# An attention and MLP kernel on one core: later hardware transposes, five output buffers, batch 2 turned by TensorE, window blocks at stride 57, and one Gelu over two tiles

## The chip, the cores and the metric

The kernel runs on one core of one Trainium2 chip. The metric is the device time of one execution in microseconds (us). Each variant was executed several times, the changed ones in the same session on the same chip as the kernel before, and only runs in the normal fast state are compared. The granted clock is the share of TensorE's full clock that the profile shows as granted. Two runs were slow and are left out: one of the kernel before (425.46 us, mean granted clock 0.749) and one of a variant (334.4 us, where its other five lie between 327.21 and 330.06).

## The reference, cut to what matters

```python
# q, k, v: 8 batches x 8 heads x 576 positions x 64, fp32
q_d, k_d, v_d = means of four neighbours of q, k, v          # 144 positions
out_up    = repeat(softmax(q_d @ k_d.T / 8) @ v_d, 4)        # coarse attention, each row four times
out_local = softmax over |i-j| < 4 only (q @ k.T / 8) @ v    # a band of 7
x = (out_up + out_local) as [8*576, 512]                     # 4608 tokens
y = gelu(x @ w_in[512, 2048]) @ w_out[2048, 512]
```

## The kernel before

The 4608 tokens are worked in nine blocks `c` of 512. `m1(c)` is x @ w_in with the Gelu (64 matmuls of 512 columns), `m2(c)` is g @ w_out (another 64), and between the matmuls of `m2(c)` the attention of batch `c+1` is woven in, so that TensorE has work while the softmax of a head pair runs on ScalarE and VectorE. I call the work from the first matmul of `m1(c)` to the first of `m1(c+1)` the stage of block c. The "opening" is everything before block 1's stage: batch 0's attention, all of block 0, and batch 1's attention within it.

```python
def m1(c):
    t = ppool.tile([128, 1024], F32, tag="nm", name="m_first")   # first two tiles: one PSUM tile
    half = [t[:, 0:512], t[:, 512:1024]]                         # (block 0 takes two separate banks)
    for fcs in ((0, 1, 2), (3,)):
        for j in range(2):
            for fc in fcs:
                nc.tensor.matmul(out=half[j], ..., start=(fc == 0), stop=(fc == 3))
                if fc == 3:
                    nc.scalar.activation(out=g[:, j, :], in_=half[j], func=ACTF.Gelu)
    for j in range(2, NJ): ...      # fourteen more tiles, in two alternating banks

def m2(c):
    for t in range(4): ...          # 16 matmuls each, then:
        osb = wpool.tile([128, 512], F32, tag="osb", bufs=2, name="out_sb")
        (VectorE or ScalarE copy)(out=osb, in_=ps)
        nc.sync.dma_start(out=out[r0:r0 + 128, :], in_=osb)

def qk_cast(b): ...   # q, k of batch b to fp16 in DRAM (two GpSimd DMAs)
def qk_turn(b): ...   # two hardware transposes ("crossbar" below) DRAM -> SBUF, on SyncE's queue; for batches >= 2
def t_in_g(b, p, which): ...   # the same by TensorE for batch 1: 6 transposes and 6 sums of four
def prep(b): ...      # VectorE: key blocks kb, sums of four kdt, kdz and qd, then v_down(b)
def v_down(b): ...    # VectorE: v summed over four neighbours (two tensor_reduce), v_lm

for c in range(NCH):
    b = c + 1
    ...               # b == 1: t_in_g between the matmuls of m1; else prep(b)
    attn(b, f2)       # f2 issues m2(c)'s matmuls in between
    qk_turn(b + 2); v_load(b + 2); qk_cast(b + 3)
    f2()              # the rest of m2(c)
# [cut: masks, the opening's plan, scores, av, norm_out]
```

In the attention of a head pair, `scores` fills a PSUM tile, ScalarE takes exp, `mask` on VectorE multiplies by the band, and only then can `av` (whose first matmul is the `sc<-e,ON` of the profile) run.

The softmax here doesn't subtract the row's maximum and nothing guards it: scores larger than these inputs give would overflow.

Of the kernel before, what the change touches and what calls it, by code (L numbers as in the profile page):

```python
# [16 lines left out]
def kernel(  # L17
# [9 lines left out]
    nc = tc.nc  # L27
# [18 lines left out]
    WN = [58 * i for i in range(5)] + [280 + 58 * i for i in range(5)]  # L46
    QN = [0, 61, 119, 177, 235, 288, 341, 399, 457, 515]
    QL = [61, 58, 58, 58, 53, 53, 58, 58, 58, 61]
# [78 lines left out]
    def vw_load(b, src, ps=None):  # L127
        for p in ps or range(NP):
            for hh in range(2):
                for g in range(2):  # L130
                    x = src[2 * p + hh, 280 * g:280 * g + 64, :]
                    nc.gpsimd.dma_start(out=ld[b % 2]["vw"][64 * hh:64 * hh + 64, 5 * g:5 * g + 5, p, 64 * hh:64 * hh + 64],  # L132
                                  in_=bass.AP(x.tensor, x.offset, [[D, 64], [58 * D, 5], [1, D]]))
# [88 lines left out]
    def m1(c):  # L222
        g = wpool.tile([128, NJ, 512], F16, tag="gT", bufs=2, name="gT")
        gT[c] = g
        x0 = 512 * c % XR
        if c:
            t = ppool.tile([128, 1024], F32, tag="nm", name="m_first")
            half = [t[:, 0:512], t[:, 512:1024]]
        else:
            half = [mm(), mm()]  # L230
        for fcs in ((0, 1, 2), (3,)):
            for j in range(2):
                for fc in fcs:
                    nc.tensor.matmul(out=half[j], lhsT=w_in_sb[:, fc, 128 * j:128 * j + 128],  # L234
                                     rhs=xT[:, fc, x0:x0 + 512], start=(fc == 0), stop=(fc == 3))
                    if fc == 3:
                        nc.scalar.activation(out=g[:, j, :], in_=half[j], func=ACTF.Gelu)  # L237
                    yield
        for j in range(2, NJ):
            ps = mm()  # L240
            for fc in range(4):
                nc.tensor.matmul(out=ps, lhsT=w_in_sb[:, fc, 128 * j:128 * j + 128],  # L242
                                 rhs=xT[:, fc, x0:x0 + 512], start=(fc == 0), stop=(fc == 3))
                if fc == 3:
                    nc.scalar.activation(out=g[:, j, :], in_=ps, func=ACTF.Gelu)  # L245
                yield

    def m2(c):
        g = gT[c]
        for t in range(4):  # L250
            r0 = 512 * c + 128 * t
            if c == NCH - 1 and t == 3:
                for half in range(2):
                    cs = slice(256 * half, 256 * half + 256)
                    ps = mm()
                    for j in range(NJ):
                        nc.tensor.matmul(out=ps[:, 0:256], lhsT=g[:, j, 128 * t:128 * t + 128],  # L257
                                         rhs=w_out_sb[:, j, cs], start=(j == 0), stop=(j == NJ - 1))
                        yield
                    osb = wpool.tile([128, 256], F32, tag="osa", bufs=2, name="out_sa")  # L260
                    nc.vector.tensor_copy(out=osb, in_=ps[:, 0:256])  # L261
                    nc.sync.dma_start(out=out[r0:r0 + 128, cs], in_=osb)
                continue
            ps = mm()
            for j in range(NJ):
                nc.tensor.matmul(out=ps, lhsT=g[:, j, 128 * t:128 * t + 128],  # L266
                                 rhs=w_out_sb[:, j, :], start=(j == 0), stop=(j == NJ - 1))
                if j == NJ - 1:
                    osb = wpool.tile([128, 512], F32, tag="osb", bufs=2, name="out_sb")
# [5 lines left out]
    def k_blocks(p, tr):  # L275
        for hh in range(2):
            r = slice(64 * hh, 64 * hh + 64)
            x = tr[r]
            nc.vector.tensor_copy(  # L279
                out=kb[r, p, :, 64 * hh:64 * hh + 64].rearrange("q (g i) c -> q g i c", g=2),  # L280
                in_=bass.AP(x.tensor, x.offset, [x.ap[0], [280, 2], [58, 5], [1, 64]]))

    def prep(b):
        kt, qt = xT_of(b, "kn"), xT_of(b, "qn")
        with nc.allow_low_precision(reason="sums of four, kept in fp16 as before"):
            for p in range(NP):
                k_blocks(p, kt[:, p, :])
# [8 lines left out]
    def t_in_g(b, p, which):  # L296
        nat = nat6(ld[b]["qn" if which == "q" else "kn"])
# [11 lines left out]
        else:  # L309
            k_blocks(p, tr)  # L310
# [26 lines left out]
    def v_down(b):  # L337
        L = ld[b % 2]
        with nc.allow_low_precision(reason="sums of four, kept in fp16 as before"):
            nc.vector.tensor_reduce(out=L["vd"][:, :, 0:64], in_=L["vt"].rearrange("p h r d -> p h d r"),  # L340
                                    axis=AX.X, op=ALU.add)
            nc.vector.tensor_reduce(out=L["vls"], in_=L["vl"].rearrange("p r d -> p d r"), axis=AX.X, op=ALU.add)
# [21 lines left out]
    def scores(b, p):  # L364
# [4 lines left out]
        for j in range(NW):  # L369
            c = 512 * (j // 5) + QN[j] - SH * (j // 5)  # L370
            nc.tensor.matmul(out=sc[:, c:c + QL[j]], lhsT=kb[:, p, j, :], rhs=(qT0 if b == 1 else xT_of(b, "qn"))[:, p, QN[j]:QN[j] + QL[j]],  # L371
                             start=True, stop=True)
# [165 lines left out]
    def v_load(b):  # L538
        vg_load(b, v[b])
        vw_load(b, v[b])  # L540
# [118 lines left out]
    vg_load(1, v[1])  # L659
    for f in range(4):  # L660
# [3 lines left out]
    qk_cast(2)  # L664
    qk_turn(2)
# [15 lines left out]
    for c in range(NCH):  # L681
        b = c + 1
        f1 = filler(m1(c)) if c else f1_0
        if b == 1:
            f1(10)
            for p in range(NP):
                t_in_g(1, p, "k")
                f1(7)
                t_in_g(1, p, "q")
                f1(4)  # L690
            k_lo()
            v_down(1)
# [3 lines left out]
        elif b < B:  # L696
# [3 lines left out]
        if b < B:  # L700
            to_exp()
            attn(b, f2)
            if b + 2 < B:
                qk_turn(b + 2)
# [3 lines left out]
        f2()  # L708

# [29 lines left out]
```

## Time and profile before

| what | value |
|---|---|
| time, median of 3 runs | 349.85 us (349.38 to 349.9) |
| profiled span, mean granted clock | 349.3 us, 0.976 |
| opening (start to block 1's first matmul) | 85.38 us |
| stage of block 1; of a later block | 35.42 us; 33.54 us |
| from block 1's first matmul to the end | 263.9 us |

The last three rows are read from the start of the first `m_first` matmul of each block in TensorE's timeline; the same rows are given for every kernel below. (The chain of waits dates the same start up to 0.2 us later, since it counts from the end of the matmul before.) The prediction shows the hole before block 1 and the stages. What it only mentions is how block 0's attention starts. These are two pieces of the chain of waits (start, length, what):

```profile
50.83 3.69 DVE v_d L340
...
56.23 2.19 DVE v_win L693
58.43 0.32 DVE e L383
```

and TensorE's own timeline at the same place, where the bracket is the idle time before the group and what ended it:

```profile
57.62 1.01 PE L266 MATMUL m_ps<-w_out_sb,gT 128*128 128x512 f16 x2 [2.38 <-DMA w_out_sb<-in_moe_w_out_dram]
58.79 0.64 PE L389 MATMUL sc<-e,ON 128*128 128x288 f16 x2 [0.16 <-DVE e L383]
```

Two things must both be there before TensorE can go on: the last piece of w_out (57.62) and the first mask (58.75). I call them the two gates. They arrive within 1.2 us of each other.

### The profile page before, as it was taken

Reading aid. Unit: us, or ns where it says so; the run is one execution under the profiler, and the core shown is the slowest. Engines: PE = TensorE matmul, PEld = TensorE weight load, DVE = VectorE, ACT = ScalarE, POOL = GpSimd, SP = SyncE. Lnnn points to the kernel's source line nnn. Section 1 sums busy time; section 2 is a strip of 40 time slices with the busy share of each in tenths; the row PEclk is TensorE's granted clock in tenths of the full one; section 3 lists DMA queues with packets and bytes.
Section 4 is the critical chain, followed back from the end, with each engine's and each line's share of the span. In section 5 each row is a group of like instructions: output and inputs, shape, how many; then the busy total and the mean of one; then the engine's idle time right before and its main releaser. Section 6 shows DMA issues by size and latency. Waiting matters only on the chain.

```text
span 349.3 us, 6169 instructions
## 1 busy us (share of the span) xinstructions
PE 321.3 (92%) x2430; PEld 170.8 (49%) x2430; DVE 211.3 (60%) x378; ACT 224.6 (64%) x403; POOL 140.4 (40%) x184
## 2 busy tenths in 40 slices
PE   8998996952999999999999999999999999999995
PEld 4873453520356445644554456446544654444444
DVE  7797477713966695779878978893798470000000
ACT  7764354705678767876887687768877886514620
POOL 8957677568468348666278037300000000000000
PEclk9999898995999999999999999999999999999999
DMA  6999999999999999999999979900200020011012
GB/s 83 162 205 137 153 152 119 169 179 165 171 157 122 210 165 132 167 200 197 111 133 169 197 74 122 212 17 0 92 30 0 2 93 30 2 60 61 0 44 78
DMA packets 156157, 39.93 MB, mean 114 GB/s; under 512 B 138080, under 2 KB 151648, under 8 KB 156128
## 3 DMA queue, kind: packets, MB, share of 16 engines
q0 software_dynamic: 122768, 23.02, 82.4%
q1 hardware_dynamic: 33360, 16.52, 21.4%
q8 instruction: 19, 0.31, 0.4%
q14 instruction: 10, 0.08, 0.1%
HBM read 46.01 MB, written 16.52 MB: 179 GB/s over the span
## 4 chain that ended last, share of the span: by engine, by line
PE 75%; DMA 10%; DVE 5%; ACT 4%; POOL 2%; SPq 2%; issue 1%; ACTq 0%; POOLq 0%
PE m_ps L242 31%; PE m_ps L266 29%; PE m_first L234 5%; DMA w_in_sb<-in_moe_w_in_dram 3%; DMA out_dram<-out_sb 3%; DMA q_nat<-in_q_dram 2%; PE sc L371 2%; PE nm L399 2%; PE sc L389 2%; SPq L155 2%; ACT gT L237 1%; DVE v_d L340 1%; DMA k_nat<-in_k_dram 1%; PE m_ps L257 1%; POOL k_nat L122 1%
## 5 line engine op out<-in xcount | busy, mean ns | idle before, releaser
L266 PE MATMUL m_ps<-w_out_sb,gT 128*128 128x512 f16 x560 | 132.3, 380 | 2.9 <-DMA w_out_sb<-in_moe_w_out_dram 2.9
L242 PE MATMUL m_ps<-xT,w_in_sb 128*128 128x512 f16 x504 | 112.9, 382 | 0.5 <-ACT gT L237 0.5
L245 ACT ACTIVATE gT<-m_ps 128x512 f16<-128x512 f32 x126 | 75.3, 597 | 41.2 <-PE m_ps L242 41.2
L132 POOL DMA_DIRECT2D v_win<-in_v_dram x112 | 78.4, 819 | 51.6 <-DMA v_grp<-in_v_dram 14.9
L242 PEld LDWEIGHTS <-w_in_sb 128*128 128x128 f16 x504 | 48.9, 98 | 65.7 <-issue 9.7
L266 PEld LDWEIGHTS <-gT 128*128 128x128 f16 x560 | 51.2, 98 | 56.3 <-issue 3.7
L414 DVE TENSOR_TENSOR xl<-nm,lr 128x576 f16<-128x576 f32 x28 | 21.2, 758 | 39.6 <-ACT lr L410 39.6
L270 ACT COPY out_sb<-m_ps 128x512 f32<-128x512 f32 x21 | 12.3, 585 | 38.0 <-PE m_ps L266 23.2
L261 DVE COPY out_sa<-m_ps 128x256 f32<-128x256 f32 x2 | 0.8, 425 | 56.3 <-PE m_ps L257 56.3
L234 PE MATMUL m_first<-xT,w_in_sb 128*128 128x512 f16 x64 | 17.8, 405 | 16.5 <-DVE up L416 11.0
L340 DVE TENSOR_REDUCE v_d<-v_grp 128x512 f16<-128x2048 f16 x7 | 25.9, 3705 | 0.2
L383 DVE TENSOR_TENSOR e<-e,band 128x576 f16<-128x576 f16 x28 | 12.6, 451 | 21.6 <-ACT e L378 21.5
L426 DVE TENSOR_TENSOR xT<-xl,up 128x576 f16<-128x576 f16 (+8 forms) x41 | 22.1, 566 | 1.0
L279 DVE COPY kb<-k_nat 64x640 f16<-64x640 f16 x48 | 20.6, 430 | 0.6
L408 ACT ACTIVATE lr<-sc 128x576 f32<-128x576 f32 x28 | 18.4, 657 | 3.2 <-PE sc L389 3.2
L409 ACT ACTIVATE lr<-lr 128x576 f32<-128x576 f32 x28 | 19.1, 682 | 0.9
L377 ACT ACTIVATE ed<-sc 128x288 f16<-128x288 f32 x28 | 11.4, 406 | 11.9 <-PE sc L371 11.9
L137 POOL DMA_DIRECT2D v_grp<-in_v_dram x7 | 10.5, 1500 | 20.0 <-DVE v_d L340 20.0
L378 ACT ACTIVATE e<-sc 128x576 f16<-128x576 f32 x28 | 18.0, 644 | 0.0
L234 PEld LDWEIGHTS <-w_in_sb 128*128 128x128 f16 x72 | 7.1, 103 | 20.9 <-DVE up L416 12.4
L416 DVE TENSOR_TENSOR up<-nm,lr 64x144 f16<-64x144 f32 x56 | 16.5, 295 | 0.4
L150 POOL DMA_DIRECT2D q<-in_q_dram x6 | 16.6, 2771 | 0.0
(181 smaller groups left out, 434.2 us busy)
## 6 DMA issues: line engine op xcount, KB each, us to landing
out_dram<-out_sb SPq DMA_DIRECT2D x35, 256.0 KB, 2.7
v_win<-in_v_dram POOLq DMA_DIRECT2D x112, 40.0 KB, 5.8
v_grp<-in_v_dram POOLq DMA_DIRECT2D x7, 512.0 KB, 12.5
k<-in_k_dram POOLq DMA_DIRECT2D x6, 576.0 KB, 8.7
q<-in_q_dram POOLq DMA_DIRECT2D x6, 576.0 KB, 11.1
w_in_sb<-in_moe_w_in_dram POOLq DMA_DIRECT2D x4, 512.0 KB, 8.7
w_out_sb<-in_moe_w_out_dram POOLq DMA_DIRECT2D x4, 512.0 KB, 8.7
old<-in_v_dram POOLq DMA_DIRECT2D x5, 128.0 KB, 6.8
```

The lines of the kernel that those rows point to most:

```text
L132: nc.gpsimd.dma_start(out=ld[b % 2]["vw"][64 * hh:64 * hh + 64, 5 * g:5 * g + 5, p, 64 * hh:64 * hh + 64], in_=bass.AP(x.tensor, x.offset, ...
L234: nc.tensor.matmul(out=half[j], lhsT=w_in_sb[:, fc, 128 * j:128 * j + 128], rhs=xT[:, fc, x0:x0 + 512], start=(fc == 0), stop=(fc == 3))
L242: nc.tensor.matmul(out=ps, lhsT=w_in_sb[:, fc, 128 * j:128 * j + 128], rhs=xT[:, fc, x0:x0 + 512], start=(fc == 0), stop=(fc == 3))
L245: nc.scalar.activation(out=g[:, j, :], in_=ps, func=ACTF.Gelu)
L266: nc.tensor.matmul(out=ps, lhsT=g[:, j, 128 * t:128 * t + 128], rhs=w_out_sb[:, j, :], start=(j == 0), stop=(j == NJ - 1))
L279: nc.vector.tensor_copy(out=kb[r, p, :, 64 * hh:64 * hh + 64].rearrange("q (g i) c -> q g i c", g=2), in_=bass.AP(x.tensor, x.offset, [x.a ...
L340: nc.vector.tensor_reduce(out=L["vd"][:, :, 0:64], in_=L["vt"].rearrange("p h r d -> p h d r"), axis=AX.X, op=ALU.add)
L378: nc.scalar.activation(out=e.rearrange("p (g c) -> p g c", g=2), in_=sc2[:, :, 0:SH], func=ACTF.Exp, scale=0.125)
L408: nc.scalar.activation(out=lr2, in_=sc2[:, :, 0:SH], func=ACTF.Ln)
L409: nc.scalar.activation(out=lr2, in_=lr2, func=ACTF.Exp, scale=-1.0)
L414: nc.vector.tensor_tensor(out=xl.rearrange("p (g c) -> p g c", g=2), in0=nm2[:, :, 0:SH], in1=lr2, op=ALU.mult)
L426: nc.vector.tensor_tensor(out=xT[:, p, y:y + z - a].rearrange("p (g r) -> p g r", r=4), in0=xl[:, a:z].rearrange("p (g r) -> p g r", r=4), ...
```

## The change

Five edits, meant to take away the hole before block 1 and small waits elsewhere: five output buffers instead of two, and the two transposes issued after a stage's four outputs; batch 2 loaded and turned by TensorE like batch 1, so that no transpose is needed that early; ten windows at stride 57 (one load for nine, one for the tenth) instead of two runs of five at stride 58; `v_down` as pairwise adds instead of reduces, key blocks copied for all head pairs at once; and one Gelu over the first two tiles of each block after the first.

```diff
-    WN = [58 * i for i in range(5)] + [280 + 58 * i for i in range(5)]
+    WN = [57 * i for i in range(9)] + [512]
     ...
-                    if fc == 3:
+                    if fc == 3 and c == 0:
                         nc.scalar.activation(out=g[:, j, :], in_=half[j], func=ACTF.Gelu)
+                    elif fc == 3 and j == 1:
+                        nc.scalar.activation(out=g[:, 0:2, :], in_=t.rearrange("p (j c) -> p j c", j=2), func=ACTF.Gelu)
     ...
-                    osb = wpool.tile([128, 512], F32, tag="osb", bufs=2, name="out_sb")
+                    osb = wpool.tile([128, 512], F32, tag="osb", bufs=5, name="out_sb")
     ...            # the last two half outputs share this tag now
     def v_down(b):
-            nc.vector.tensor_reduce(out=L["vd"][:, :, 0:64], in_=L["vt"].rearrange("p h r d -> p h d r"), ...)
-            nc.vector.tensor_reduce(out=L["vls"], in_=L["vl"].rearrange("p r d -> p d r"), ...)
+        for x, o in (heads 0-3, heads 4-7, v_lo):        # [shortened]
+            nc.vector.tensor_tensor(out=t, in0=x[:, :, 0:2, :], in1=x[:, :, 2:4, :], op=ALU.add)
+            nc.vector.tensor_tensor(out=o, in0=t[:, :, 0, :], in1=t[:, :, 1, :], op=ALU.add)
     ...
-    qk_cast(2)
-    qk_turn(2)
+    run(load_qk(2))
     ...
-        if b == 1:
+        if b <= 2:
             ...      # t_in_g between the matmuls of m1, k_lo, v_down
-                qk_turn(b + 2)
                 v_load(b + 2)
             ...
         f2()
+        if b + 2 < B:
+            qk_turn(b + 2)
```

More of the change, by code (lines that the diff above doesn't have):

```diff
@@ L45 @@
     NW = 10
-    WN = [58 * i for i in range(5)] + [280 + 58 * i for i in range(5)]
-    QN = [0, 61, 119, 177, 235, 288, 341, 399, 457, 515]
-    QL = [61, 58, 58, 58, 53, 53, 58, 58, 58, 61]
+    WN = [57 * i for i in range(9)] + [512]
+    QN = [0] + [57 * i + 3 for i in range(1, 10)]
+    QL = [60] + [57] * 8 + [60]
     SH = S // 2
@@ L127, in vw_load, with vw_last @@
     def vw_load(b, src, ps=None):
+        vw = ld[b % 2]["vw"]
         for p in ps or range(NP):
             for hh in range(2):
-                for g in range(2):
-                    x = src[2 * p + hh, 280 * g:280 * g + 64, :]
-                    nc.gpsimd.dma_start(out=ld[b % 2]["vw"][64 * hh:64 * hh + 64, 5 * g:5 * g + 5, p, 64 * hh:64 * hh + 64],
-                                  in_=bass.AP(x.tensor, x.offset, [[D, 64], [58 * D, 5], [1, D]]))
+                x = src[2 * p + hh, 0:64, :]
+                nc.gpsimd.dma_start(out=vw[64 * hh:64 * hh + 64, 0:9, p, 64 * hh:64 * hh + 64],
+                                    in_=bass.AP(x.tensor, x.offset, [[D, 64], [57 * D, 9], [1, D]]))
+    def vw_last(b, src):
+        for hh in range(2):
+            nc.gpsimd.dma_start(out=ld[b % 2]["vw"][64 * hh:64 * hh + 64, 9, :, 64 * hh:64 * hh + 64],
+                                in_=src[hh:H:2, 512:576, :].rearrange("h s d -> s h d"))
     def vg_load(b, src):
@@ L259, in m2 @@
                         yield
-                    osb = wpool.tile([128, 256], F32, tag="osa", bufs=2, name="out_sa")
+                    osb = wpool.tile([128, 512], F32, tag="osb", bufs=5, name="out_sb")[:, 0:256]
                     nc.vector.tensor_copy(out=osb, in_=ps[:, 0:256])
@@ L272, in m2, with k_blocks @@
                 yield
-    def k_blocks(p, tr):
+    def k_blocks(ps, tr):
         for hh in range(2):
             r = slice(64 * hh, 64 * hh + 64)
+            o = kb[r, ps, :, 64 * hh:64 * hh + 64]
             x = tr[r]
-            nc.vector.tensor_copy(
-                out=kb[r, p, :, 64 * hh:64 * hh + 64].rearrange("q (g i) c -> q g i c", g=2),
-                in_=bass.AP(x.tensor, x.offset, [x.ap[0], [280, 2], [58, 5], [1, 64]]))
+            nc.vector.tensor_copy(out=o[:, :, 0:9, :], in_=bass.AP(x.tensor, x.offset, [x.ap[0], x.ap[1], [57, 9], [1, 64]]))
+            nc.vector.tensor_copy(out=o[:, :, 9, :], in_=x[:, :, 512:576])
     def prep(b):
@@ L285, in prep @@
         with nc.allow_low_precision(reason="sums of four, kept in fp16 as before"):
-            for p in range(NP):
-                k_blocks(p, kt[:, p, :])
+            k_blocks(slice(0, NP), kt)
             nc.vector.tensor_reduce(out=kdt, in_=kt.rearrange("p a (g r) -> p a g r", r=4), axis=AX.X, op=ALU.add)
@@ L296, in t_in_g @@
     def t_in_g(b, p, which):
-        nat = nat6(ld[b]["qn" if which == "q" else "kn"])
+        nat = nat6(ld[b % 2]["qn" if which == "q" else "kn"])
         trf = ppool.tile([128, 1024], F32, tag="sc", bufs=2, name=f"tg_{which}")
@@ L309, in t_in_g @@
         else:
-            k_blocks(p, tr)
+            k_blocks(slice(p, p + 1), tr[:, 0:S].unsqueeze(1))
             for hh in range(2):
@@ L338, in v_down @@
         L = ld[b % 2]
-        with nc.allow_low_precision(reason="sums of four, kept in fp16 as before"):
-            nc.vector.tensor_reduce(out=L["vd"][:, :, 0:64], in_=L["vt"].rearrange("p h r d -> p h d r"),
-                                    axis=AX.X, op=ALU.add)
-            nc.vector.tensor_reduce(out=L["vls"], in_=L["vl"].rearrange("p r d -> p d r"), axis=AX.X, op=ALU.add)
+        for x, o in ((L["vt"][:, 0:4], L["vd"][:, 0:4, 0:64]), (L["vt"][:, 4:8], L["vd"][:, 4:8, 0:64]),
+                     (L["vl"].unsqueeze(1), L["vls"].unsqueeze(1))):
+            n = o.shape[1]
+            t = wpool.tile([128, S + 2 * Sd], F32, tag="lr", bufs=2, name="v_two")
+            t = t[:, 0:128 * n].rearrange("p (h r d) -> p h r d", h=n, r=2)
+            nc.vector.tensor_tensor(out=t, in0=x[:, :, 0:2, :], in1=x[:, :, 2:4, :], op=ALU.add)
+            nc.vector.tensor_tensor(out=o, in0=t[:, :, 0, :], in1=t[:, :, 1, :], op=ALU.add)
         nc.vector.tensor_tensor(out=L["vlm"][:, :, 0:64], in0=L["vls"].unsqueeze(1).broadcast_to([128, H, 64]),
@@ L370, in scores @@
             c = 512 * (j // 5) + QN[j] - SH * (j // 5)
-            nc.tensor.matmul(out=sc[:, c:c + QL[j]], lhsT=kb[:, p, j, :], rhs=(qT0 if b == 1 else xT_of(b, "qn"))[:, p, QN[j]:QN[j] + QL[j]],
+            nc.tensor.matmul(out=sc[:, c:c + QL[j]], lhsT=kb[:, p, j, :], rhs=(qT0 if b <= 2 else xT_of(b, "qn"))[:, p, QN[j]:QN[j] + QL[j]],
                              start=True, stop=True)
@@ L539, in v_load @@
         vg_load(b, v[b])
+        vw_last(b, v[b])
         vw_load(b, v[b])
@@ L659 @@
     vg_load(1, v[1])
+    vw_last(1, v[1])
     for f in range(4):
@@ L683 @@
         f1 = filler(m1(c)) if c else f1_0
-        if b == 1:
+        if b <= 2:
             f1(10)
             for p in range(NP):
-                t_in_g(1, p, "k")
+                t_in_g(b, p, "k")
                 f1(7)
-                t_in_g(1, p, "q")
+                t_in_g(b, p, "q")
                 f1(4)
             k_lo()
-            v_down(1)
+            v_down(b)
+        if b == 1:
             nc.vector.memset(ld[0]["vw"].rearrange("p j a d -> p (j a d)").bitcast(F32), 0.0)
@@ L695 @@
             qk_cast(3)
-        elif b < B:
+        elif 2 < b < B:
             prep(b)
```

## The prediction

> **What bounds the kernel now.** I read the page first (busy shares, the forty slices), then the chain of waits in order of time, then TensorE's timeline where that chain leaves TensorE, then the ScalarE, SyncE and VectorE timelines at those places, and last the table by stages.
>
> ```profile
> PE 321.3 (92%) x2430; PEld 170.8 (49%) x2430; DVE 211.3 (60%) x378; ACT 224.6 (64%) x403; POOL 140.4 (40%) x184
> PE   8998996952999999999999999999999999999995
> ```
>
> TensorE is the bound: 321.3 of 349.3 us, and in the second line there is one hole, in the ninth and tenth slices (5 and 2, about 70 to 87 us). The 28 us in which TensorE does nothing are all that a change without less TensorE work can win. The chain of waits passes through the hole like this:
>
> ```profile
> 69.34 0.76 DVE xl L414
> 70.32 0.31 DVE up L416
> 70.63 5.73 SPq L155
> 76.41 5.22 DMA out_dram<-out_sb
> 81.77 0.44 issue
> 82.21 0.67 ACT lr L408
> ...
> 85.38 3.06 PE m_first L234 x7
> 88.46 0.61 ACT gT L237
> 89.11 0.38 PE m_first L234
> 89.48 12.09 PE m_ps L242 x56
> ```
>
> Two hardware transposes hold SyncE's queue (L155), the first output transfers stand behind them, and ScalarE waits for an output buffer; only then do the last normalisation (L408), xT and the next block's first matmuls follow. Three single timelines give the same hole its size:
>
> ```profile
> 85.38 3.05 PE L234 MATMUL m_first<-xT,w_in_sb 128*128 128x512 f16 x7 [10.70 <-DVE up L416]
> ```
> ```profile
> 81.73 0.58 ACT L270 COPY out_sb<-m_ps 128x512 f32<-128x512 f32 x1 [11.95 <-DMA out_dram<-out_sb]
> ```
> ```profile
> 63.94 6.15 SPq L155 DMA_TRANSPOSE k_nat<-k  x1
> 70.25 6.10 SPq L155 DMA_TRANSPOSE q_nat<-q  x1
> 76.41 6.26 SPq L271 DMA_DIRECT2D out_dram<-out_sb  x3
> ```
>
> TensorE waits 10.70 us, because ScalarE waited 11.95 us for a buffer whose transfer began only at 76.41. Note too that batch 2's transposes end at about 76.4, while its preparation would be wanted at 74.7 if there were no hole: taking away only the buffer wait would leave a wait for the transposes. The seven matmuls after the hole take 3.05 us, the same seven 1.68 us in a later stage. From the third block on every stage looks like this one:
>
> ```profile
> 151.27 3.24 PE m_ps L266 x15
> 154.51 1.57 PE m_first L234 x7
> 156.11 0.61 ACT gT L237
> 156.75 0.38 PE m_first L234
> 157.13 12.09 PE m_ps L242 x56
> ```
> ```profile
> 154.50:188.10 33.60, 32.91 (x246) 17.26 (x244) 28.20 (x42) 26.31 (x49) 20.85 (x27) 1.00 1.46 150
> ```
>
> The eighth m_first matmul waits for the Gelu over the seven before it, though it writes another bank: both halves are one tile. The table by stages says the same: 33.60 us long, 32.91 busy, and the missing 0.69 is exactly TensorE's wait before that matmul. This happens in the eight blocks after the first. In a stage DVE has 28.2 of 33.6 us and ACT 26.3, so neither binds.
>
> [...] outputs that were ready waited behind two transposes of 6.15 and 6.10 us. [...] The trace has 406 ns for exp over 288 elements and 644 for 576, which is 0.83; so a Gelu over 1024 instead of 512 elements costs 597 + 512 * 0.83 = 1.02 us (estimate). [...] the strided v_d reduce takes 3705 ns for 2048 inputs[...]. [...] kb copies between SBUF take 324 ns, but one of them 4.03 us while GpSimd issued loads.
>
> **The change part by part.**
>
> *Output buffers and crossbar.* Five buffers instead of two and transposes behind the four outputs of a stage: the wait of 10.70 us has no cause left. In the first block there is now no transpose ahead of the outputs at all. The cold restart goes with it: 3.05 - 1.68 = 1.37. At the next border TensorE's wait of 0.35 (at 120.80, from the same buffers) should go as well. Sum -12.4 us. I take the full 10.70, since without the ScalarE wait the chain L408 to xT ends as in later stages, where xT arrives before TensorE needs it.
>
> *Batch 2 like batch 1.* 96 small matmuls are added to TensorE's stage of block 1. What a set of twelve (six transposes, six sums of four) displaces is read from the chain in batch 1: m_ps L242 x7 begins at 41.29 and lasts 1.52, the next begins at 43.21, hence 0.40 for the twelve between. Eight sets: +3.2 us, on TensorE and therefore in full on the path. VectorE per head pair: two 9-window copies at about 0.46 (the 576-wide qT copy from the same memory took 458 ns), two 64-wide ones at 0.20, kdz 0.62, qT and qd 0.76: 2.7 us, against 11 * 0.216 + 0.80 = 3.2 us of TensorE. It stays hidden, narrowly. It replaces the two reduces of 2.55, kdz 0.64 and kb 2.66 of that batch.
>
> *One Gelu.* 0.69 goes away eight times. Against it: the Gelu over both tiles starts 0.22 later than the first one did and lasts 1.02, so the next Gelu ends about 0.1 us after TensorE wants its bank for the fifth tile (the third and fourth tile take 0.86 each). Net 0.59 * 8 = -4.7 us.
>
> *v_down and prep.* The 3.70 and 0.58 us reduces become six tensor_tensor operations: 2 * 0.69 (512 wide, fp32 out, like v_lm's 693 ns) + 2 * 0.42 + 0.29 + 0.22 = 2.7, less some overlap: about 1.8 us off VectorE per batch. The eight kb copies become four. In a steady stage both lie beside TensorE and are worth nothing. Only in block 0 does VectorE's v_down lie on the chain (50.83 to 58.43, ending in the mask of 0.32), but there TensorE also waits 2.38 us for the last piece of w_out at 57.62. With the mask earlier, w_out alone decides. Its place in the queue's bytes is nearly unchanged; but window loads are 10 issues instead of 16 per batch, and in the issue order each load from GpSimd waits for the eighth before it, so the last piece can be issued some 2.5 us earlier than 49.79. The DMA engines are over 90% busy there, so I count only -0.7 (estimate, +0.3 to -2).
>
> *Stride 57.* Same number of windows, same 576 columns: nothing on TensorE.
>
> Sum: -12.4 + 3.2 - 4.7 - 0.7 = -14.6; 349.85 - 14.6 = 335.2 us.
>
> **The rivals.**
>
> First: the wait moves to batch 2's loads. Twelve issues at 0.80 us follow the last window load at about 55, so they are issued by about 66 and landed by about 70 to 72; k, the last, is wanted after ten matmuls of block 1, at about 76.5. For it speaks that the DMA engines are full until 75 us; against it that in the kernel before the same bytes (k and q cast) took from 57.5 to 69, with transposes beside them that now vanish. If late by 4 us: about 339.
>
> Second: VectorE becomes the bound of block 1's first half. [...] batch 1's took 0.99 a pair under full GpSimd issue. If a head pair took 3.7 instead of 2.7, TensorE would lose 4 * 0.5 = 2 us: 337.
>
> Third: the later transposes come too late, for batch 3 above all. Its cast is issued after v_load(2), at about 80; landed about 90 to 95; transposes until about 103; wanted at about 110 (74.5 + 36). In the kernel before, one batch of loads took about 26 us of GpSimd's time (81.08 to 107.35), a stage takes 33: the slack grows. A miss would show as a wait at the third block's start and cost 3 to 6 us.
>
> Fourth: the Gelu wait is merely moved, to the fifth tile: then only 2 us of the 4.7 would come, about 338. Against it: ScalarE idles 0.27 us per tile there and 0.49 us before the first Gelu.
>
> **Range and chances.** The hole (-12.4, surely over -10), the added matmuls (+3 to +4.5) and the Gelu (-3 to -5.5) give -8.5 to -16, and w_out a little more. Two rivals at once would make 341. Range 332 to 339.5. The border of 2% is 342.9; to miss it half the hole would have to return as another wait. Faster 0.95, same 0.04, slower 0.01.
>
> **What would show it.** The hole of 10.70 us is gone and m_first of block 1 begins at about 74.5 with at most 0.5 us of wait; ScalarE's wait for an output transfer vanishes; on SyncE's queue four outputs stand before the first transpose. Twice as many tg_k and tg_q matmuls, block 1's stage about 36.2 us long, blocks 2 to 6 about 33.0 each instead of 33.55, m_first as eight in a row (1.9 us) with a Gelu of about 1.0 us after it. I am wrong if TensorE waits for k_nat or q_nat's DMA in block 1, for tg copies by VectorE, at block 2's start for transposes, or more than 0.2 us at the fifth tile's first matmul.

## The result, and the profile after

The changed kernel took 331.70 us (median of 4, 331.24 to 332.28) against 349.88 us (349.38 to 351.62) for the kernel before: ratio 0.9473, 95% interval 0.9437 to 0.9509. Ratios here are the mean time of one kernel's fast runs over that of the other's in the same rounds, so they are not quite the ratio of the medians quoted. Two repetitions gave 0.9472 and 0.9497 (332.25 and 332.91 us). The result is correct. The direction was predicted; the gain, 18.2 us, is 3.6 us more than the predicted 14.6, and the time lies just below the predicted range of 332.0 to 339.5; the two repetitions lie just inside it.

The page of the changed kernel, busy times and TensorE's forty slices:

```profile
PE 319.2 (97%) x2526; PEld 172.7 (52%) x2526; DVE 198.5 (60%) x414; ACT 222.6 (67%) x395; POOL 121.7 (37%) x152
PE   8988897999999999999999999999999999999996
```

The hole (the slices 5 and 2) is gone, and TensorE is busy 97% of the span although it has 96 more matmuls. The chain of waits around block 1 (start, length, what):

```profile
69.02 3.24 PE m_ps L273 x15
72.26 1.73 PE m_first L239 x8
73.99 0.43 PE m_ps L249 x2
74.42 0.26 PE tg_k L307 x6
...
108.18 1.73 PE m_first L239 x8
109.91 12.12 PE m_ps L249 x56
```

Before, this chain left TensorE for the normalisation, SyncE's queue and an output transfer; now it goes from the last matmuls of block 0 straight into block 1, whose `m_first` are eight in a row, with batch 2's small matmuls (`tg_k`) among the rest. The table by stages of the same kernel (stretch: its length, then the busy time of PE, PEld, DVE, ACT and POOL, then granted clock, DMA share, GB/s) shows the stages of blocks 1 and 2:

```profile
72.26:108.18 35.92, 35.92 (x341) 20.40 (x340) 24.35 (x69) 25.73 (x47) 21.50 (x23) 1.00 1.90 158
108.18:140.88 32.70, 32.70 (x245) 17.21 (x244) 22.12 (x41) 25.62 (x47) 13.02 (x15) 1.00 1.70 177
```

Length and busy time agree to the hundredth: TensorE waits for nothing. On SyncE's queue the four outputs now stand before the first transpose:

```profile
61.13 12.18 SPq L278 DMA_DIRECT2D out_dram<-out_sb  x4
80.73 6.32 SPq L160 DMA_TRANSPOSE k_nat<-k  x1
87.16 7.12 SPq L160 DMA_TRANSPOSE q_nat<-q  x1
```

and ScalarE's timeline has one Gelu of 1024 columns, with TensorE's eighth matmul as its releaser and no wait for an output transfer ahead of it:

```profile
72.36 0.59 ACT L277 COPY out_sb<-m_ps 128x512 f32<-128x512 f32 x1
74.02 1.02 ACT L244 ACTIVATE gT<-m_first 128x1024 f16<-128x1024 f32 x1 [1.07 <-PE m_first L239]
```

The opening's two gates, in TensorE's timeline, moved from 57.62 and 58.79 to:

```profile
54.91 0.59 PE L273 MATMUL m_ps<-w_out_sb,gT 128*128 128x512 f16 x2 [1.79 <-DMA w_out_sb<-in_moe_w_out_dram]
55.92 0.64 PE L398 MATMUL sc<-e,ON 128*128 128x288 f16 x2 [0.42 <-DVE e L392]
```

The span fell from 349.3 to 330.3 us, by 19.0. By parts, read as in the table before: opening 85.38 to 72.10 (-13.28), block 1's stage 35.42 to 35.92 (+0.50), everything after it 228.50 to 222.28 (-6.22). The opening's fall is more than its hole of 10.70: the stretch with the two gates is 1.43 us shorter, and another 1.83 us come from the stretch before it, where seven matmuls at 36 us ran at a slow clock in the profile before (granted clock 0.62, 2.57 us) and not in this one (1.00, 1.67 us). A repetition of the changed kernel has that slow stretch too (2.43 us; see "The opening" below), so the 1.83 us can't be put down to the change.

### The profile page after: what moved, and what is told of

It reads as the page before. It is cut to its first block, busy times and chain, and to the rows that moved or that the text cites. A ratio compares the mean times of both kernels' runs of the same rounds, so it can differ in the third digit from the quotient of the medians.

```text
span 330.3 us, 6291 instructions
## 1 busy us (share of the span) xinstructions
PE 319.2 (97%) x2526; PEld 172.7 (52%) x2526; DVE 198.5 (60%) x414; ACT 222.6 (67%) x395; POOL 121.7 (37%) x152
## 4 chain that ended last, share of the span: by engine, by line
PE 86%; POOL 5%; DMA 5%; DVE 2%; issue 1%; POOLq 0%; DVEq 0%
PE m_ps L273 36%; PE m_ps L249 32%; PE m_first L239 4%; DMA w_in_sb<-in_moe_w_in_dram 3%; PE nm L408 3%; PE sc L380 2%; PE sc L398 2%; DMA k_nat<-in_k_dram 1%; POOL old L174 1%; PE nm L405 1%; PE nm L404 1%; PE m_ps L264 1%; PE sc L376 1%; POOL k_nat L122 1%; POOL k_nat L168 1%; DVE v_win L704 1%
## 5 line engine op out<-in xcount | busy, mean ns | idle before, releaser
L249 PEld LDWEIGHTS <-w_in_sb 128*128 128x128 f16 x504 | 48.0, 97 | 56.6 <-issue 1.8
L132 POOL DMA_DIRECT2D v_win<-in_v_dram x56 | 44.0, 824 | 19.3 <-DMA v_grp<-in_v_dram 10.0
L268 DVE COPY out_sb<-m_ps 128x256 f32<-128x256 f32 x2 | 0.8, 425 | 54.8 <-PE m_ps L264 54.8
L137 POOL DMA_DIRECT2D v_win<-in_v_dram x14 | 9.8, 787 | 48.0 <-PE nm L408 47.6
L239 PE MATMUL m_first<-xT,w_in_sb 128*128 128x512 f16 x64 | 15.1, 379 | 0.0
L244 ACT ACTIVATE gT<-m_first 128x1024 f16<-128x1024 f32 x8 | 8.2, 1024 | 8.7 <-PE m_first L239 8.7
L155 POOL DMA_DIRECT2D q<-in_q_dram x5 | 13.9, 2782 | 0.0
L142 POOL DMA_DIRECT2D v_grp<-in_v_dram x7 | 9.5, 1351 | 10.9 <-DVE v_two L350 10.9
L420 ACT ACTIVATE lr<-lr 64x288 f32<-64x288 f32 x28 | 12.4, 443 | 0.9
```

The lines of the kernel that those rows point to most:

```text
L132: nc.gpsimd.dma_start(out=vw[64 * hh:64 * hh + 64, 0:9, p, 64 * hh:64 * hh + 64], in_=bass.AP(x.tensor, x.offset, [[D, 64], [57 * D, 9], [ ...
L155: nc.gpsimd.dma_start(out=t, in_=src[b].rearrange("h s d -> s h d"))
L239: nc.tensor.matmul(out=half[j], lhsT=w_in_sb[:, fc, 128 * j:128 * j + 128], rhs=xT[:, fc, x0:x0 + 512], start=(fc == 0), stop=(fc == 3))
L249: nc.tensor.matmul(out=ps, lhsT=w_in_sb[:, fc, 128 * j:128 * j + 128], rhs=xT[:, fc, x0:x0 + 512], start=(fc == 0), stop=(fc == 3))
```

## The experiments

The theory after the result: (1) the hole is worth about 12 us, (2) batch 2 on TensorE costs about 3.2, (3) the second Gelu's wait is worth more than its idle time, (4) the opening's new loads and adds give something, up to 2. The rivals: the Gelu was as predicted and the opening gave the rest; or the hole was worth more than 12; or batch 2's rerouting is itself needed for the gain. All of this table is from the profiles, each a single execution; "late" is the stage of a block after block 1, and "rest" runs from block 1's first matmul to the end.

| kernel | opening | block 1 | late | rest |
|---|---|---|---|---|
| before | 85.38 | 35.42 | 33.54 | 263.9 |
| before + one Gelu | 83.14 | 34.45 | 32.72 | 258.3 |
| before + five buffers | 72.43 | 35.19 | 33.53 | 263.7 |
| before + both | 72.91 | 37.17 | 32.72 | 259.9 |
| after (and two repetitions) | 72.10 (73.29, 71.71) | 35.92 | 32.70 | 258.2 |
| after, two Gelus | 70.16 | 36.77 | 33.51 | 264.6 |
| after, two Gelus, both late | 74.03 | 35.92 | 32.76 | 258.6 |
| after, old windows | 73.25 | 35.95 | 32.73 | 258.4 |
| after, old v_down | 72.75 | 35.92 | 32.70 to 32.80 | 258.5 |
| after, both old | 72.76 | 35.95 | 32.72 | 258.3 |
| after, two buffers | 72.07 | 36.03 | 32.70 | 258.3 |
| after, batch 2 by crossbar (and a repetition) | 71.00 (71.80) | 32.69 | 32.70 | 255.3 |
| the same, w_out first | 69.88 | 34.23 | 32.70 | 256.8 |
| the same, w_out first and memset later | 68.60 | 35.35 | 32.70 | 258.0 |

All kernels gave the correct result.

### One Gelu alone

```diff
 # kernel before
-                    if fc == 3:
+                    if fc == 3 and c == 0:
                         (Gelu of tile j)
+                    elif fc == 3 and j == 1:
+                        (one Gelu over both tiles)
```

> The kernel before with only the Gelu change: one Gelu over both first tiles in blocks 1 to 8. Theory R (refill): the wait before the eighth m_first matmul costs its idle time of 0.69 us and also the refilling of TensorE's pipeline, 0.38 - 0.216 = 0.17 us, which the profile books as busy; so a stage shrinks from 33.55 to about 32.70 us, eight times 0.86: 349.9 - 6.9 = 343.0 us. Theory P (the prediction): 0.59 us per block, 345.2 us, and the other 0.27 us per stage seen in the changed kernel comes from another part (stride, buffers, lighter VectorE); then stages are about 32.96 us here.

Measured 345.74 us (343.13 to 346.99) against 350.58: 0.9863 (0.9813 to 0.9913). A late stage fell from 33.54 to 32.72, that is by 0.82 rather than 0.59, and the rest by 5.6 us, less than eight times that because in two stages (33.29 and 33.28) TensorE now waits 0.40 us, once at the border for VectorE's last `up` and once within the stage for a mask; with five buffers as well (below) no later stage has such a wait. The hole stays, as TensorE's timeline shows:

```profile
83.14 3.59 PE L234 MATMUL m_first<-xT,w_in_sb 128*128 128x512 f16 x8 [10.03 <-DVE up L418]
```

The timed gain of 4.8 us is smaller than the profile's 7.9 (its execution was the fastest of the four), because the opening varies by itself, as shown below. By the total time alone theory P (345.2 us) would have been the nearer one; the length of the stages, 32.72 against its 32.96, speaks for theory R (32.70).

### The changed kernel with two Gelus, and with two Gelus issued together

```diff
 # a_two_gelus: the condition as before
-                    if fc == 3 and c == 0:
+                    if fc == 3:
                         (Gelu of tile j)
-                    elif fc == 3 and j == 1: (one Gelu over both tiles)
 # a_two_gelus_late: two Gelus, both behind the eighth matmul
                     elif fc == 3 and j == 1:
-                        (one Gelu over both tiles)
+                        for i in range(2):
+                            nc.scalar.activation(out=g[:, i, :], in_=half[i], func=ACTF.Gelu)
```

> The changed kernel with the two separate Gelus of before. Theory R: +6.9 us, 338.6 us, stages back to about 33.55 us with 0.69 idle. Theory P: +4.7 us, 336.4 us, stages of 33.3 us.

> The changed kernel with two Gelus of 512 elements, but both issued after the eighth m_first matmul, so that no matmul waits between. Theory R says that only the wait counts and not the number of Gelus: 331.7 to 332.5 us, no idle time before the eighth matmul, and the third Gelu starts about 0.1 us later than with the single one. Rival: the single, longer ScalarE instruction is what saves; then this lies halfway back, 334 us or more.

Measured, against 350.58: 337.81 us (336.42 to 339.8), ratio 0.965 (0.9601 to 0.9699), and 333.88 us (332.35 to 334.56), ratio 0.9519 (0.9478 to 0.9561). The chain of waits of the first:

```profile
107.09 1.52 PE m_first L239 x7
108.61 0.02 issue
108.64 0.60 ACT gT L242
109.24 0.04 issue
109.29 0.38 PE m_first L239
109.66 3.45 PE m_ps L247 x16
```

From the first of the eight to the ninth matmul these are 2.57 us; in the changed kernel the same eight take 1.73 (108.18 to 109.91). The 0.84 us between them are more than the wait of 0.69 that the timeline brackets show. The table by stages of this kernel says where the rest is booked:

```profile
106.93:140.43 33.50, 32.81 (x245) 17.18 (x244) 22.10 (x41) 25.88 (x48) 13.14 (x15) 1.00 1.78 180
```

33.50 long and 32.81 busy with the same 245 matmuls that are busy for 32.70 in the changed kernel. So this wait inside a stream of matmuls costs a stage its idle time of 0.69 and another 0.11 that the profile counts as busy: a lone matmul shows its full 0.38 us, one in a stream adds 0.216 (12.12 / 56). These two would make 0.16. That is what the two waits of 0.40 in the kernel with one Gelu show (stages of 33.28 against 32.72, busy for 32.88 against 32.72), and 0.15 is what the 0.84 has beyond 0.69; where the stage here wins back the rest was not traced. Over the eight blocks the two kernels' rests differ by 6.4 us. The third kernel shows that the size of the instruction is not what counts: two Gelus that both start after the eighth matmul cost 0.06 per stage more than one, as no matmul waits for them. The timed difference between the two variants (3.9 us) is less than the stages say (6.0); in the profiled executions (336.84 and 334.56) this is because their openings, 70.16 and 74.03, differ the other way. For the same reason the time of 333.88 falls between the two forecasts for the third kernel, and only its stages decide.

### Five buffers alone

```diff
 # kernel before
-                    osb = wpool.tile([128, 256], F32, tag="osa", bufs=2, name="out_sa")
+                    osb = wpool.tile([128, 512], F32, tag="osb", bufs=5, name="out_sb")[:, 0:256]
-                    osb = wpool.tile([128, 512], F32, tag="osb", bufs=2, name="out_sb")
+                    osb = wpool.tile([128, 512], F32, tag="osb", bufs=5, name="out_sb")
```

(The two half-width outputs take two of the same five buffers, as in the change.)

> The kernel before with only five output buffers (the last two half outputs take two of the same five [...]); transposes and batch 2 as before. Theory B: ScalarE's wait for a buffer is the whole cause of the hole; batch 2's transposes end at about 76.4 us and VectorE can work on keys first, so block 1 starts at about 74.7 and nothing waits: 349.9 - 12.4 = 337.5 us. Theory X (said in the prediction): without the buffer wait a wait for the transposes is left, the scores of batch 2 come late and TensorE loses 3 us or more of it again: 340.5 us or more.

Measured 338.58 us (337.77 to 340.5) against 350.58: 0.9676 (0.9635 to 0.9717), a gain of 12.0, between the two forecasts and nearer to theory B. Five buffers alone remove the whole hole, although batch 2's transposes still stand before the first outputs. The remaining wait for the transposes, which the prediction feared here, is there on VectorE (its timeline first), but most of it does not reach TensorE (the last line):

```profile
75.04 2.89 DVE L279 COPY kb<-k_nat 64x640 f16<-64x640 f16 x8 [2.20 <-DMA k_nat<-k]
77.95 2.55 DVE L288 TENSOR_REDUCE kdt<-k_nat 128x576 f16<-128x2304 f16 x1
80.53 3.87 DVE L291 COPY kdz<-kdt 64x576 f16<-64x576 f16 x2
...
87.50 3.70 DVE L340 TENSOR_REDUCE v_d<-v_grp 128x512 f16<-128x2048 f16 x1
```
```profile
92.85 0.41 PE L389 MATMUL sc<-e,ON 128*128 128x288 f16 x2 [1.49 <-DVE e L383]
```

VectorE starts 2.20 us late, takes 3.87 us for two copies of which one alone took 3.47, where the median over all batches is 0.31 (what held it is not shown; in the kernel before, a kb copy of 4.03 us among the eight from 188.27 on ran while GpSimd issued loads, 187.62 to 192.15), and the mask comes 1.49 us late. Block 1's stage is 35.19 against 33.53, so 1.66 us are lost in place of the hole of 10.70.

### Five buffers and one Gelu

The two edits above together, in the kernel before.

> The kernel before with only five buffers and the single Gelu. If the two terms add: the 338.9 us of the five buffers alone, less 8 * 0.83 = 6.6 us: 332.2 us, no slower than the whole change by more than 1 us, since its other parts are then -2.5 us in the opening and +3.2 us for batch 2 on TensorE. If they overlap (the Gelu's gain in block 1 is eaten by the late mask there, 1.49 us with five buffers alone): 333.5 us or more.

Measured 334.68 us (332.63 to 336.46) against 350.4: 0.955 (0.9508 to 0.9593), in the same session as a repetition of the changed kernel (below) at 332.91. Two small edits give 15.7 of its 17.5 us. They overlap, as the second forecast (333.5 or more) had it. What is missing sits in block 1, 37.17 us against a late stage of 32.72: TensorE reaches the mask 0.8 us earlier, the preparation of batch 2 does not get ready earlier, and the wait for the mask grows to 2.60 us:

```profile
93.62 0.40 PE L391 MATMUL sc<-e,ON 128*128 128x288 f16 x2 [2.60 <-DVE e L385]
```

The chain of waits shows what followed this wait. The next nine matmuls of `m2` after it, and the same nine of the next head pair:

```profile
94.57 3.63 PE m_ps L268 x9
...
99.83 1.94 PE m_ps L268 x9
```

The first nine took 3.63 us and the second nine 1.94, so the first ran at 0.53 of the rate of the second (1.94 / 3.63) and cost 1.69 us more: 2.60 + 1.69 are 4.29 of the 4.45 us.

### Two buffers in the changed kernel

```diff
 # changed kernel
-                    osb = wpool.tile([128, 512], F32, tag="osb", bufs=5, name="out_sb")
+                    osb = wpool.tile([128, 512], F32, tag="osb", bufs=2, name="out_sb")   # and the half outputs
```

> The changed kernel with two output buffers instead of five. Theory B2 (either the buffers or the absence of transposes ahead of the outputs removes the hole; the order of the crossbar is then enough): 332 to 333 us, no wait of ScalarE for an output transfer over 1 us. Rival: the buffers are needed also here, because block 0's outputs land late among the loads: ScalarE waits for a buffer in block 0 or 1 and TensorE loses over 2 us, 334 us or more.

Measured 332.29 us (330.27 to 333.62) against 350.96: 0.9463 (0.9426 to 0.95), the same as the changed kernel's ratio within the interval. ScalarE waits for an output transfer once, 0.99 us in block 2's stage, and TensorE does not notice (block 1's stage 36.03, the later ones 32.70). So the hole had one mechanism, outputs stuck behind transposes with too few buffers, and either half of the cure is enough: buffers, or no transpose ahead of the outputs.

### Batch 2 by the crossbar again

```diff
 # changed kernel
-    run(load_qk(2))
+    qk_cast(2)
+    qk_turn(2)
-        if b <= 2:
+        if b == 1:
-        elif 2 < b < B:
+        elif 1 < b < B:
     ...            # and scores takes batch 2's q from the crossbar's tile
```

> The changed kernel with batch 2 cast and turned by the crossbar as in the kernel before (the transposes again ahead of block 0's outputs, but five buffers). Theory B (the buffers alone removed the hole; the 96 matmuls for batch 2 are 3.2 us of pure cost): block 1's stage falls from 35.9 to 32.7 us, 3.2 us faster than the changed kernel of this call, about 328.5 us. Theory X (the transposes of batch 2 come too late without the hole): VectorE starts its preparation late, TensorE waits for the scores or the mask of batch 2, and the time is as long as that of the changed kernel or longer.

> The changed kernel with batch 2 through the crossbar once more, as the reference for the next two and to see that its gain repeats: 328 to 329 us, block 1's stage 32.7 us, no TensorE wait in block 1.

Measured 328.47 us (fast runs 327.21 to 330.06) against 350.37, ratio 0.9368 (0.9338 to 0.9398), and in another session 327.17 us (326.56 to 329.07) against 350.96, ratio 0.9334 (0.9305 to 0.9363). This is faster than both kernels of the study. Batch 2's transposes stand before the outputs once more (SyncE's queue):

```profile
60.67 6.08 SPq L160 DMA_TRANSPOSE k_nat<-k  x1
66.91 6.23 SPq L160 DMA_TRANSPOSE q_nat<-q  x1
73.19 2.11 SPq L278 DMA_DIRECT2D out_dram<-out_sb  x4
```

and VectorE waits for them, but with five buffers nobody needs the outputs, and TensorE's chain is whole. VectorE's line, then the chain:

```profile
73.32 3.00 DVE L287 COPY kb<-k_nat 64x2304 f16<-64x2304 f16 x1 [1.90 <-DMA k_nat<-k]
```
```profile
71.16 1.73 PE m_first L239 x8
72.89 12.12 PE m_ps L249 x56
...
103.86 1.73 PE m_first L239 x8
```

Block 1 takes 32.69 us like any other stage. The same late transposes cost 1.66 us with the old preparation, 4.45 (1.69 of it in the nine slow matmuls of that execution) with the old preparation and one Gelu, and nothing with the preparation of the change. From the end of its wait to the end of v_lm VectorE needs 14.2 us here and 17.4 in the kernel with five buffers. The adds save 1.5 of this, and the copies to kb and kdz, one of which is long in either kernel (kb 3.00 here, one kdz copy there), another 1.5. Which part of the change brings the latter, the merged copies or the fewer loads from GpSimd, no run separates.

### The opening: old windows, old v_down, both

```diff
 # a_old_windows: windows at 58, five per load, 16 loads per batch; stride 57 and vw_last taken out
 # a_reduce: v_down with its two tensor_reduce as before
 # a_old_both: both
```

> The changed kernel unaltered, as the reference for the three others of this call on the same chip. 331 to 333 us. In the opening (before block 1's first matmul, at 72.26 us in its first profile) both theories allow another clock draw: if the seven matmuls after batch 1's first key transposes run cold (2.5 to 3.1 us instead of 1.67), this profile's block 1 starts 1 to 1.5 us later.

> The changed kernel with the old windows: stride 58 in two groups of five, sixteen window loads per batch instead of ten. Theory L (fewer, larger loads let the last piece of w_out be issued earlier): it is issued at about 47.5 instead of 44.7 us, lands 1 to 2 us later, and the kernel is 1 to 2 us slower than the changed kernel of this call. Theory N (the early gain was a draw of clock and transfers): within 0.5 us of it. Both: no wait elsewhere, stages 32.7 us.

> The changed kernel with v_down as the two reduces of before. Theory G (two gates: in block 0 TensorE needs both the last w_out piece and VectorE's mask, and in the changed kernel the mask is the later one by 0.42 us): the mask comes about 1.7 us later, at about 57.3 us, TensorE waits about 2 us for it, +1.7 us. The prediction's claim that w_out alone decides there: within 0.5 us. Stages stay at 32.7 us in both.

> The changed kernel, reference for the two others of this call: 331.5 to 332.5 us.

> The changed kernel with the old windows and the old v_down together. Theory G (two gates of one wait, the later decides): about as slow as with the old v_down alone, +2 to +3.5 us on the reference, about 335 us. Theory A (two separate gains that add): +4.5 to +5.5 us, about 337 us. Theory N2 (the early gain is only a draw of the clock): within 1 us of the reference.

| kernel | us, median (range) | before, same session | ratio |
|---|---|---|---|
| after, repeated | 332.25 (330.25 to 333.74) | 350.37 | 0.9472 (0.9439 to 0.9504) |
| old windows | 333.95 (331.55 to 335.94) | 350.37 | 0.9523 (0.9485 to 0.9561) |
| old v_down | 336.24 (333.12 to 337.18) | 350.37 | 0.9572 (0.9534 to 0.9609) |
| after, second repetition | 332.91 (331.19 to 333.79) | 350.4 | 0.9497 (0.946 to 0.9534) |
| both old | 333.11 (331.64 to 334.82) | 350.4 | 0.9512 (0.9471 to 0.9552) |

With the old windows, the w_out piece is the late gate again (TensorE's timeline):

```profile
53.18 1.02 PE L268 MATMUL m_ps<-w_out_sb,gT 128*128 128x512 f16 x4 [1.78 <-DMA w_out_sb<-in_moe_w_out_dram]
...
56.82 1.01 PE L268 MATMUL m_ps<-w_out_sb,gT 128*128 128x512 f16 x2 [2.20 <-DMA w_out_sb<-in_moe_w_out_dram]
```

and with the old v_down it is the mask:

```profile
56.45 0.64 PE L395 MATMUL sc<-e,ON 128*128 128x288 f16 x2 [1.82 <-DVE e L389]
```

In the changed kernel's profile these two waits are 1.79 and 0.42. In four of the eight profiles named below TensorE waits at the last piece of w_out and not at the mask, in the other four at both. From block 0's first `m2` matmul to that first `sc<-e,ON` the four profiles of kernels built on the one before have 7.99 to 8.73 us (mean 8.35); the eight with both new parts and the change's own order of loads have 6.33 to 7.42 (mean 6.67); old windows 8.78, old v_down 7.86, both old 7.86. So the two parts together are worth 1.2 to 1.7 us (against both old, or against the kernels built on the one before), and neither alone gives more than a third of it: the later gate decides. These are single executions.

In the total time this can hardly be seen. Old windows is 1.7 us worse with overlapping intervals, old v_down 4 us, but both old only 0.2 (where theory N2 had put it), and these can't all be the price of the same lines. The opening varies by itself. Small waits for pieces of k stand among batch 1's first transposes, and the matmuls after them run fast in one execution of the changed kernel and slow in another. The first kind, then the second, each from TensorE's timeline of the same kernel:

```profile
36.51 1.67 PE L249 MATMUL m_ps<-xT,w_in_sb 128*128 128x512 f16 x7
```
```profile
36.19 2.43 PE L249 MATMUL m_ps<-xT,w_in_sb 128*128 128x512 f16 x7
```

The seven matmuls took 1.67 or 2.43 to 3.13 us over all profiles, of either kernel. From the first transpose of batch 1 to block 0's first `m2` matmul, the three executions of the changed kernel need 15.44, 17.13 and 14.71 us. The granted clock in the seven matmuls is 1.00 in the first profile of the changed kernel (1.67 us) and 0.62 in that of the kernel before (2.57 us). This is not chance alone: over all seventeen profiles the four with slow matmuls are the four in which the waits for k before them add up to most, 1.58 to 1.73 us against 0.32 to 1.36.

A second such place follows the gates. From the first `sc<-e,ON` to block 1's start it is 14.75 us in three profiles (two Gelus, crossbar, w_out first), where the next nine matmuls of `m2` took 2.10 us, and 16.2 to 16.4 in eight others, where they took 2.89 to 3.58; in the changed kernel, one of the eight (16.18 us), the granted clock in the 4 us from 55.92 on was 0.62. Here the waiting before does not tell them apart: in the 5 us before, TensorE was busy 2.94 us in "w_out first" and 2.92 in the crossbar's repetition, and the nine matmuls took 2.10 us in the one and 3.01 in the other.

In the timed runs of the first repetition, the run at mean clock 0.999 took 330.25 and one at 0.988 took 333.40. How the opening's gain divides in total time therefore stays open.

### Starting block 1 earlier

```diff
 # x_wout_first: batch 2 by crossbar, and in the opening
     for f in range(4):
         (load piece f of w_out)
-        vw_load(1, v[1], [f])
+    vw_load(1, v[1])
 # x_both: that, and v_win's memset with v_load(2) and qk_cast(3) behind it moved behind batch 1's second mask
```

> The reference of this call with all four pieces of w_out issued before the first nine-window loads of batch 1 (the order of issues alone is changed). Theory G (two gates in block 0: the last w_out piece and VectorE's mask): the wait for w_out of 1.5 to 2.1 us vanishes, but TensorE then waits for the mask at about 55.5 us; gain at most 0.5 us. The prediction's claim that w_out alone decides there: 2 to 2.5 us faster, about 326 us.

> As the run before, and the clearing of batch 2's window tile (2.19 us on VectorE) moved behind the first two masks, with the loads that need it. Theory G: both gates go, block 0's weighted sums start about 2 us earlier[...]: 325.5 to 326.5 us. If w_out alone decides: the same as the run before.

Measured, against 350.96 and with the crossbar variant at 327.17 in the same session: 329.12 us (328.43 to 329.76), ratio 0.9378 (0.9352 to 0.9403), and 328.26 us (328.06 to 329.94), ratio 0.9366 (0.9338 to 0.9393). Neither gains, and theory G's forecast for the second, 325.5 to 326.5, did not come. In the first the wait for w_out is gone and the mask holds TensorE instead, as theory G said (TensorE's timeline):

```profile
55.13 0.40 PE L398 MATMUL sc<-e,ON 128*128 128x288 f16 x2 [2.06 <-DVE e L392]
```

In the second, both gates are open and the first `sc<-e,ON` runs at 52.58, some 3 us earlier than in the crossbar variant (55.50 in its repetition). Block 1 starts at 68.60. But batch 2's transposes end no earlier, and TensorE pays it back in block 1:

```profile
85.12 0.28 PE L376 MATMUL sc<-qd,kdz 128*128 128x144 f16 x2 [1.21 <-DVE qd L298]
...
89.21 0.41 PE L398 MATMUL sc<-e,ON 128*128 128x288 f16 x2 [1.13 <-DVE e L392]
```

Opening and block 1 together are 103.95 us (104.11 in the first), against 103.69 and 104.50 in the two crossbar profiles. In these two runs batch 2's transposes and the preparation behind them set the time there, not the opening.

## Why the prediction was right or wrong

**The hole, -12.4: right.** The waits of 10.70 and 0.35 and the slow restart (seven matmuls in 3.05 us at a granted clock of 0.54) are gone: in the changed kernel block 1's first eight take 1.89 us. Five buffers alone gave 12.0 in timed runs, with a new loss of 1.66 in block 1's stage and the variation of the opening in it. The remark that the transposes' wait would remain if only the buffers were mended was right for VectorE (2.20 us) and too dark for TensorE (1.66 us).

**Batch 2 on TensorE, +3.2: right in size, and pure cost.** 35.92 - 32.70 = 3.22 us. VectorE took 2.66 us a head pair (its seven copies from 74.85 on; 2.7 were estimated) and stayed hidden. What I had not asked is whether the step was needed: with the crossbar kept, the hole stays closed and 3.8 to 5.1 us are gained in time (medians of 328.47 against 332.25 in one session, 327.17 against the 332.29 of the two-buffer kernel in the other).

**One Gelu, -4.7: the step that failed; its mechanism was right, its size was not.** "Net 0.59 * 8 = -4.7 us" took the 0.69 that the timeline shows as idle for the whole price and subtracted 0.1 for a new wait at the fifth tile. Measured, a stage loses 0.80 to 0.82 us: 0.69 idle plus about 0.11 booked as busy; and the fifth tile waits for nothing (35.92 and 32.70 busy of as much). The 1024-wide Gelu itself took 1.02 us as estimated. Eight blocks make -6.5 rather than -4.7. The prediction's own range for this term (-3 to -5.5) did not hold it. This is 1.8 of the 3.6 us by which the sum was off.

**The opening, -0.7: too small, for a wrong step.** "With the mask earlier, w_out alone decides" is half of it. The order of issues that the step used is in GpSimd's timeline of the kernel before: the loads at 41.48, 44.68, 48.49 and 54.04 were issued after waits of 2.52, 1.86, 0.27 and 2.12 us, each for the load eight before it. But both gates are close, w_out alone decides in four of eight profiles and the mask comes last in the other four, and each of the old versions makes its own gate the last. The last piece of w_out was in hand 2.7 us earlier (54.91 against 57.62), not less than a microsecond. Within the segment the two parts are worth 1.2 to 1.7 us.

**v_down and the block copies, "worth nothing in a steady stage": right there** (32.70 to 32.80 with the old v_down), **but they matter where batch 2 is prepared by VectorE.** With them the preparation takes 14.2 instead of 17.4 us, and the crossbar version loses nothing in block 1; 1.5 us of the difference are the adds, the rest is not separated.

**The sum.** -12.4 + 3.2 - 6.5 - 1.7 = -17.4 us, that is 332.5 from 349.85, with the larger figure for the opening; measured 331.7, 332.25 and 332.91. The rest of under 1 us is within the 1.6 us by which the opening varied between executions of the changed kernel, and that the first measurement fell just below the range while its repetitions fell inside is luck. **The rivals** did not come: no wait for batch 2's loads, for VectorE in block 1, or for batch 3's transposes (they end at 94.3, wanted from 108).

## What to carry to other kernels

Price a wait inside a matmul stream by the length of the whole stage with and without it, not by the idle time in the bracket, and move the instruction that makes the next matmul wait rather than making it shorter. Where one wait has two causes, try each cure alone before paying for both: here buffers cost nothing, while rerouting batch 2 cost 3.2 us of the bound engine and was not needed. When two gates stand close together, expect little from opening one, and when a stage starts earlier, look first at what it will wait for next.

## What this case measured of the hardware

- A lone matmul of 512 columns took 0.38 us, and one in a stream 0.216 (12.12 us for 56). What a wait in mid-stream costs beyond its idle time would be the difference of the two, 0.16 us (an estimate); measured, it was 0.16 at each of the two waits of 0.40 in the kernel with one Gelu, and 0.11 of a stage's 0.80 at the second Gelu's.
- At 36 us, seven matmuls took 2.43 to 3.13 us in the four profiles in which several short waits before them added up to 1.58 us or more, and 1.67 in the thirteen with 1.36 or less. After block 0's gates nine matmuls took 3.01 us in one execution and 2.10 in another, after nearly the same waiting (TensorE busy for 2.92 and 2.94 of the 5 us before). One wait of 2.60 us was followed by nine matmuls that took 1.69 us longer than the nine of the next head pair, and the opening varied between executions of the changed kernel by 1.6 us. What sets the clock in these places is not shown.
- A load of ScalarE's activation table took 1283 ns (mean of the groups in the kernel before). In the changed kernel one began 0.02 us after the activation before it had ended (70.82 to 70.84), and the next activation began at its end (72.13).
- A strided tensor_reduce of 2048 inputs took 3705 ns where a contiguous one of 2304 takes 2553; two rounds of pairwise adds did its work in 2.21 us (0.69 + 0.42 + 0.68 + 0.42). Why the strided one is slower is not shown.
